# Block-sparse attention and mixture of experts: two loads and stores issued from another queue, and an exponential that permutes while it reads

## The chip, the cores and the metric

The kernel runs on one core of one Trainium2 chip. The metric is the time of one execution on the device in microseconds (us); smaller is better. Every time below comes from runs on the chip or from the trace of one profiled execution.

## The reference

Two computations in a row. First an attention over blocks of 32 positions, with a mask made of a window, the first and last block, and three blocks drawn for each query block; then a layer in which each of the 3072 tokens goes through one of eight experts. All is fp32.

```
B, H, S, D = 4, 8, 768, 64;  block = 32;  n_blocks = 24
mask = |blk_i - blk_j| <= 1, or blk_i or blk_j is the first or the last block
mask[qb*32:(qb+1)*32, kb*32:(kb+1)*32] = True  for the 3 sampled kb of each qb
scores = where(mask, q @ k^T / sqrt(D), -1e9) - max
attn = exp(scores);  attn /= attn.sum + 1e-9;  attn = attn @ v
x = attn as (3072 tokens, 512)
logits = x @ w_gate + modality_bias[modality_id];  e = argmax;  gate_w = softmax(logits)[e]
out = gate_w * (relu(x @ w1[e]) @ w2[e])          # w1 512x1024, w2 1024x512
```

## The kernel before

**Stages.** Up to about 250 us runs the attention, after that the experts, in groups of 256 tokens. The attention has dense rows (first and last query block, lines 360 to 450) and 22 sparse steps: a step g = half*11 + m takes two batches ("half") and the query blocks 2m+1 and 2m+2, and works through items ("s", half, m, n, b), n the query block of the two and b the batch of the two.

**One item** is a chain over four engines. `scores` (L505, TensorE) multiplies 32 queries with eight key blocks: window, first and last, and three drawn ones. `masked` (L513, VectorE) adds the mask and finds the row's minimum, into `y` and `mn`. `exps` (L521, ScalarE) computes exp in two calls of 256 columns, into `a`. `transposed` (L531, TensorE) turns `a` in pieces of 128 columns, and `copied` (L536) brings them out of PSUM. `weigh_shared` (L553) multiplies with the v blocks that both query blocks of the step see, `weigh_own` (L562) with those of one query block alone, the drawn ones among them. `divide` (L435 to L437, VectorE) writes the token rows `xr`; `turned` (L569, L571) and `gate` (L579, L582) make the logits, and `write` (L317, L322) puts `xr` with its gate sum into the DRAM tensor `x_d`, from which the experts gather their tokens later.

**Order of columns.** `y` holds, per half c of 128 columns, the columns in the order (s, f): slot s of four key blocks, position f of 32. v lies on the partitions in the order (f, s), since `vbuf` is viewed as `"(f s) c x -> f s c x"`. Somewhere between, (s, f) has to become (f, s); that happens in `exps`.

**Loads.** Everything from DRAM is fetched ahead by hand. SyncE (SP in the profile) issues `fetch_v` (L479: v of the first and last block, in the first two steps of a half; L480, L481: v of window blocks, 256 KB each), `fetch_own` (L490 reads the drawn block numbers into registers, L493 then issues six loads of 128 KB a step), `dense_q`, `dense_k`, `dense_v` (L146, L153, L159), the experts' weights (L682, L686), `fetch_q` (L141, `q_raw`, one 256 KB load a step, three buffers) and the `x_d` stores of `write` (L322, two of 256.5 KB a step). L322's rows come from `xr` in sparse steps and from `xrd` in dense ones.

**What sets the order.** The order on each engine is the order in which the code is run: a list START for the beginning, then a loop over ticks in which each item's operations come LAG ticks after its start; loads are hooked in at fixed places (`KL`, `QP`, `VL`, `VG`). `write` is a generator that is advanced a little each tick; LATER = 15 idle advances lie between its reciprocal (L317) and its two stores (L322). An engine runs its instructions in order; one that waits holds all behind it.

**Completion semaphores.** A transfer issued by SP or ACT signals its landing on one of eight semaphores, DMAHW0 to DMAHW7, which are given out in turn over both queues. The next transfer on the same semaphore carries a wait for the landing of the one before, whichever queue that was issued from. In the rows of order below, `[waits DMAHW6_49]` is such a wait; PE, DVE and Pool in these brackets stand for results of those engines.

Of the kernel before, what the change touches and what calls it, by code (L numbers as in the profile page):

```python
# [20 lines left out]
P = 128  # L21
# [66 lines left out]
def attention_moe(ctx, tc, kD, qD, qH, v0, v1, blocks, modality, w_gate, bias, w1, w2, out):  # L88
    nc = tc.nc
# [4 lines left out]
    x_d = dram.tile([NTOK, HD + 1], F32, name="x_d")  # L94
# [22 lines left out]
    with ExitStack() as actx:  # L117
# [20 lines left out]

        def fetch_q(half, m):
            q_raw = work.tile([P, 2, HB * NPAIR * 32], F32, name="q_raw", bufs=3)  # L140
            nc.sync.dma_start(q_raw.rearrange("p n f -> p (n f)"), qH[half, m])  # L141
            return q_raw.rearrange("p n (u q) -> p u n q", q=32)

        def dense_q(half):
# [165 lines left out]
        def write(tau, xrs):  # L310
            gs = small.tile([P, 2], F32, name="gs")
            nc.vector.tensor_reduce(gs, exs.pop(tau), axis=AX.X, op=ALU.add)
            yield
            nc.vector.tensor_scalar(gs, gs, 1e-9, None, ALU.add)
            yield
            for n in range(2):
                nc.vector.reciprocal(xrs[n][:, HD:HD + 1], gs[:, n:n + 1])  # L317
            yield
            for _ in range(LATER):
                yield  # L320
            for n in range(2):
                nc.sync.dma_start(x_d[(tau + n) * P:(tau + n + 1) * P, :], xrs[n])  # L322

        def rank(t0_, t1_):
            n = t1_ - t0_
# [192 lines left out]
        def exps(total, y, mn):  # L518
            a = work.tile([P, 768], F32, name="a", bufs=5)[:, 0:512].rearrange("p (u k) -> p u k", u=2)
            for u in range(2):  # L520
                nc.scalar.activation(a[:, u, :].rearrange("p (c f s) -> p c s f", c=2, s=4), y[:, u, :].rearrange("p (c s f) -> p c s f", c=2, s=4),  # L521
                                     AF.Exp, bias=mn[:, u:u + 1], scale=-1.0, accum_out=total[:, u:u + 1])
            return a

# [64 lines left out]
        def routing(tau, lg, pair):  # L589
            yield from route(tau, lg, pair)  # L590
            if tau + 2 < NT:
                yield from write(tau, pair)
                yield from chain(tau + 2)
                return
            both = [chain(tau + 2), write(tau, pair)]
            while both:
                for g in list(both):
                    try:
                        yield next(g)
                    except StopIteration:  # L600
                        both.remove(g)
# [485 lines left out]
        xrs, turns, banks, sums, ats, gated = {}, {}, {}, {}, {}, set()  # L1087
# [19 lines left out]
        for k, it in enumerate(sparse[0] + sparse[1]):  # L1107
            items.append(it)
            if k in DENSE_AFTER:
                c = 2 * DENSE_AFTER.index(k)  # L1110
# [38 lines left out]
        def q_load(m, half):  # L1149
            qraw[m, half] = fetch_q(half, m)  # L1150
# [9 lines left out]
        for g in range(2 * NM):  # L1160
            half, m = divmod(g, NM)
# [19 lines left out]
        def do(op, it):  # L1181
# [29 lines left out]
            else:  # L1211
# [6 lines left out]
                elif op == "M":  # L1218
                    st[it] = masked(m, n, b, st[it])
                elif op == "X":  # L1220
                    if (n, b) == (0, 0):
                        sums[m, half] = small.tile([P, 4, 2], F32, name="sums", bufs=4)
                    st[it] = exps(sums[m, half][:, 2 * b + n, :], *st[it])
                elif op == "T":
                    st[it] = transposed(n, st[it])
                elif op == "A":
                    if n == 0:
                        ats[m, half, b] = work.tile([P, 16, 2, 32], F32, name="at", bufs=NAT)
                    copied(n, b, st.pop(it), ats[m, half, b])
                    if (n, b) == (1, HB - 1):  # L1230
                        sums[m, half] = spread(sums[m, half])
                elif (n, b) == (1, HB - 1):
                    if op == "W":
                        st[it] = bank()
                        weigh_shared(half * NM + m, st[it], [ats[m, half, b_] for b_ in range(HB)])
                    elif op == "V":
                        banks[m, half] = bank()
                        sum_rows(sums.pop((m, half)), banks[m, half])
                        weigh_own(half * NM + m, st[it], [ats[m, half, b_] for b_ in range(HB)])
                    elif op == "O":  # L1240
                        new_tile(m, half)
                        divide(st.pop(it), banks.pop((m, half))[:, 0:H], slice(0, P), H, xrs[m, half][:, 0:HD])
                    elif op == "Y":
                        turns[m, half] = turned(xrs[m, half])
                    elif op == "G":
                        end_tile(m, half)
# [94 lines left out]
```

## Time and profile before

| | |
|---|---|
| median of 3 runs | 559.29 us (558.52 to 562.44) |
| the profiled execution | 560.91 us |
| its span, first to last instruction | 559.2 us |
| mean granted TensorE clock | 0.980 |
| TensorE (PE) busy | 519.0 us, 93% |
| VectorE (DVE) busy | 370.7 us, 66% |
| ScalarE (ACT) busy | 348.2 us, 62% |
| GpSimd (POOL) busy | 182.7 us, 33% |
| DMA traffic | 124.68 MB, 223 GB/s on average |

The span lies inside the execution; 1.7 us are outside it. Times in the profile count from the span's start. SyncE has no row of busy time, as it only issues transfers; its rows are named SPq, and the length of such a row is the time that the queue took to issue the transfer, not the time until the data has landed.

### The profile page before, as it was taken

To read this page: it belongs to the slowest core of one execution; us is meant where nothing else is said; L and a number is where in the kernel's file an instruction comes from. 1 tells how busy PE (TensorE), PEld (TensorE's weight loads), DVE (VectorE), ACT (ScalarE), POOL (GpSimd) and SP (SyncE) were. 2 spreads that over 40 slices of the span, in tenths; PEclk is the share of its full clock that TensorE was granted. 3 is DMA by queue.
4 is the path that set the end of the run, shared out by engine and by line. 5 is a ranking of instruction groups with operands and counts; after the bars stand their busy time and mean duration, and the time that the engine had idled before them with its cause. 6 is when DMAs were issued, how large, how long until landed. Compare 5 with 4: busy or idle time off the path is not lost.

```text
span 559.2 us, 18870 instructions
## 1 busy us (share of the span) xinstructions
PE 519.0 (93%) x7274; PEld 435.4 (78%) x7274; DVE 370.7 (66%) x1151; ACT 348.2 (62%) x746; POOL 182.7 (33%) x413
## 2 busy tenths in 40 slices
PE   6899989999889986889999999999999999999992
PEld 4577767677667664679888898989989899898971
DVE  4796767687678874976986556655566555665560
ACT  3789966987868965862564545545455454554560
POOL 1745526352546542403334330320303203032030
PEclk9999989999999996989999999999999999999997
DMA  8865878777657768857677975767757567575720
GB/s 281 296 197 188 278 227 260 248 248 255 192 163 211 211 193 295 249 169 264 201 239 251 308 250 186 263 193 240 238 190 260 194 228 246 194 259 190 236 105 22
DMA packets 48691, 124.68 MB, mean 223 GB/s; under 512 B 7376, under 2 KB 7504, under 8 KB 48592
## 3 DMA queue, kind: packets, MB, share of 16 engines
q1 hardware_dynamic: 44512, 110.26, 61.4%
q0 software_dynamic: 4080, 13.12, 6.5%
q8 instruction: 59, 0.97, 0.7%
q14 instruction: 40, 0.33, 0.2%
HBM read 110.76 MB, written 12.86 MB: 221 GB/s over the span
## 4 chain that ended last, share of the span: by engine, by line
PE 76%; DVE 7%; DMA 5%; issue 4%; SPq 3%; ACT 2%; POOL 1%; POOLq 0%; DVEq 0%
PE bank L731 8%; PE bank L714 8%; PE bank L730 8%; PE bank L729 8%; PE bank L715 8%; PE bank L716 8%; PE bank L505 7%; PE bank L531 6%; DMA slot<-v 4%; PE bank L553 3%; PE bank L562 3%; PE bank L579 2%; PE bank L703 2%; DVE y L513 1%; PE bank L569 1%
## 5 line engine op out<-in xcount | busy, mean ns | idle before, releaser
L691 DVE TENSOR_TENSOR slot<-slot 128x1024 fp32r<-128x1024 f32 x96 | 120.8, 1264 | 102.8 <-ACT slot L690 98.2
L690 ACT CAST slot<-slot 128x1024 fp32r<-128x1024 f32 x104 | 108.0, 1049 | 109.4 <-PE bank L731 47.1
L521 ACT ACTIVATE a<-y,mn 128x256 f32<-128x256 f32 x176 | 119.5, 779 | 5.2 <-DVE mn L513 5.1
L714 PE MATMUL bank<-slot 128*128 128x256 f32 x384 | 108.4, 282 | 0.0
L716 PE MATMUL bank<-slot 128*128 128x256 f32 x384 | 107.7, 281 | 0.0
L715 PE MATMUL bank<-slot 128*128 128x256 f32 x384 | 107.6, 280 | 0.0
L740 POOL DMA_INDIRECT out<-slot,si x21 | 21.2, 1011 | 182.5 <-ACT slot L736 179.4
L731 PE MATMUL bank<-slot 128*128 128x512 f32 x200 | 79.2, 396 | 1.1 <-DVE slot L722 1.1
L729 PE MATMUL bank<-slot 128*128 128x512 f32 x200 | 80.0, 400 | 0.0
L730 PE MATMUL bank<-slot 128*128 128x512 f32 x200 | 79.1, 395 | 0.0
L469 POOL COPY slot<-slot 128x128 f32 x264 | 64.5, 300 | 26.8 <-issue 26.7
L714 PEld LDWEIGHTS bank<-slot 128*128 128x128 f32 x384 | 72.2, 188 | 0.6
L715 PEld LDWEIGHTS bank<-slot 128*128 128x128 f32 x384 | 72.1, 188 | 0.5
L716 PEld LDWEIGHTS bank<-slot 128*128 128x128 f32 x384 | 72.2, 188 | 0.0
L513 DVE CUSTOM_DVE_ANT_1 y<-bank,smask 128x256 f32<-128x256 f32 x176 | 66.3, 417 | 1.3 <-PE bank L505 0.6
L531 PE MATMUL bank<-ident,a 128*128 128x128 f32 x352 | 54.7, 284 | 6.1 <-DVE mn L513 5.6
L505 PE MATMUL bank<-slot,q_raw 64*32 64x256 f32 x1408 | 51.4, 388 | 3.3 <-DMA q_raw<-qH 2.6
L531 PEld LDWEIGHTS bank<-ident,a 128*128 128x128 f32 x352 | 38.7, 142 | 12.2 <-DVE mn L513 5.0
L731 PEld LDWEIGHTS bank<-slot 128*128 128x128 f32 x200 | 37.6, 188 | 11.0 <-DVE slot L722 2.0
L536 ACT COPY at<-bank 128x512 f32<-128x512 f32 x66 | 38.8, 589 | 9.7 <-PE bank L531 9.6
L730 PEld LDWEIGHTS bank<-slot 128*128 128x128 f32 x200 | 37.6, 188 | 8.1 <-DVE slot L691 0.4
L729 PEld LDWEIGHTS bank<-slot 128*128 128x128 f32 x200 | 37.6, 188 | 7.8 <-ACT slot L889 0.3
(290 smaller groups left out, 817.2 us busy)
## 6 DMA issues: line engine op xcount, KB each, us to landing
slot<-w SPq DMA_DIRECT2D x105, 512.0 KB
slot<-v SPq DMA_DIRECT2D x140, 128.0 KB
slot<-v SPq DMA_DIRECT2D x44, 256.0 KB
slot<-v SPq DMA_DIRECT2D x8, 768.0 KB
x_d<-xr SPq DMA_DIRECT2D x22, 256.5 KB
q_raw<-qH SPq DMA_DIRECT2D x22, 256.0 KB
slot<-kD SPq DMA_DIRECT2D x7, 768.0 KB
x_d<-xrd SPq DMA_DIRECT2D x2, 256.5 KB
```

What stands on the lines that cost most here:

```text
L505: nc.tensor.matmul(sp[u][32 * pr:32 * pr + 32, b * 256:(b + 1) * 256], lhsT=q[r, b * NPAIR + pr, n, :], rhs=kv[r, s0:s0 + 8, b, pr, :], st ...
L513: nc.vector.tensor_tensor_reduce(y[:, u, :].rearrange("p (s f) -> p s f", s=8), sp[u][:, b * 256:(b + 1) * 256].rearrange("p (s f) -> p s ...
L521: nc.scalar.activation(a[:, u, :].rearrange("p (c f s) -> p c s f", c=2, s=4), y[:, u, :].rearrange("p (c s f) -> p c s f", c=2, s=4), AF. ...
L531: nc.tensor.transpose(tp[:, k:k + P], a[:, u, c * P:(c + 1) * P], ident)
L690: nc.scalar.copy(h, staged(n))
L691: (eng or (nc.gpsimd if n in POOL_SPLITS else nc.vector)).tensor_tensor(l, staged(n), h.bitcast(F32), ALU.subtract)
L714: nc.tensor.matmul(o, lhsT=h[:, fs], rhs=xh[g % 2][:, c, :], start=c == 0 and f % 2 == 0, stop=False)
L715: nc.tensor.matmul(o, lhsT=h[:, fs], rhs=xl[g % 2][:, c, :], start=False, stop=False)
L716: nc.tensor.matmul(o, lhsT=l[:, fs], rhs=xh[g % 2][:, c, :], start=False, stop=c == 3 and f % 2 == 1)
L729: nc.tensor.matmul(o, lhsT=hh[0][:, f, ts_], rhs=h[:, fs], start=f == 0, stop=False)
L730: nc.tensor.matmul(o, lhsT=hh[0][:, f, ts_], rhs=l[:, fs], start=False, stop=False)
L731: nc.tensor.matmul(o, lhsT=hl[f // 4][:, f % 4, ts_], rhs=h[:, fs], start=False, stop=f == 7)
```

## The change

Three lines. `fetch_q` issues its 22 loads of `q_raw` from ScalarE's queue (`nc.scalar`) and no longer from SyncE's; `write` does the same with its 24 stores into `x_d`. `exps` makes the order (f, s) on its input: it now reads `y` with a step of 32 elements (every slot's element f, then the next f) and writes `a` in one run, where before it read `y` in one run and wrote `a` with a step of four elements. 176 instructions have this form.

```diff
@@ def fetch_q(half, m):
-            nc.sync.dma_start(q_raw.rearrange("p n f -> p (n f)"), qH[half, m])
+            nc.scalar.dma_start(q_raw.rearrange("p n f -> p (n f)"), qH[half, m])
@@ def write(tau, xrs):
             for n in range(2):
-                nc.sync.dma_start(x_d[(tau + n) * P:(tau + n + 1) * P, :], xrs[n])
+                nc.scalar.dma_start(x_d[(tau + n) * P:(tau + n + 1) * P, :], xrs[n])
@@ def exps(total, y, mn):
-                nc.scalar.activation(a[:, u, :].rearrange("p (c f s) -> p c s f", c=2, s=4), y[:, u, :].rearrange("p (c s f) -> p c s f", c=2, s=4),
+                nc.scalar.activation(a[:, u, :].rearrange("p (c f s) -> p c f s", c=2, s=4), y[:, u, :].rearrange("p (c s f) -> p c f s", c=2, s=4),
                                      AF.Exp, bias=mn[:, u:u + 1], scale=-1.0, accum_out=total[:, u:u + 1])
```

The instructions of TensorE, VectorE and GpSimd keep their order. On SyncE's and ScalarE's queues three places show what moves.

**Place A, near 60 us.** SyncE before, the loads of own v (L493) and window v (L480, L481) around the first two stores:

```order
L493 DMA slot<-v 32x1024 [waits DMAHW0_49]
L493 ISA
L493 DMA slot<-v 32x1024 [waits DMAHW1_49]
L493 ISA
L493 DMA slot<-v 32x1024 [waits DMAHW2_49]
L480 DMA slot<-v 32x2x1024 [waits DMAHW3_49,PE_49]
L481 DMA slot<-v 32x2x1024 [waits DMAHW4_49]
L322 DMA x_d<-xrd 128x513 [waits DMAHW5_49,DVE_49]
L322 DMA x_d<-xr 128x513 [waits DMAHW6_49,DVE_49]
L141 DMA q_raw<-qH 128x512 [waits DMAHW7_49]
```

SyncE after, the same L493 group and the one before it:

```order
L480 DMA slot<-v 32x2x1024 [waits DMAHW4_49,PE_49]
L481 DMA slot<-v 32x2x1024 [waits DMAHW5_49]
L490 TENSOR_LOAD rb_i
L493 ISA
L493 DMA slot<-v 32x1024 [waits DMAHW6_49]
L493 ISA
L493 DMA slot<-v 32x1024 [waits DMAHW7_49]
L493 ISA
L493 DMA slot<-v 32x1024 [waits DMAHW0_49]
L146 DMA qd<-qD 128x512 [waits DMAHW1_49]
L153 DMA slot<-kD 128x1536 [waits DMAHW2_49]
```

ScalarE after, where before the row of L571 was followed by four of L521 with no transfer among them:

```order
L571 COPY xT<-bank 128x512 [waits PE_49]
L521 ACTIVATE a,sums<-y,mn 128x256 [waits DVE_49] x2
L322 DMA x_d<-xrd 128x513 [waits DMAHW6_49,DVE_49]
L322 DMA x_d<-xr 128x513 [waits DMAHW7_49,DVE_49]
L141 DMA q_raw<-qH 128x512 [waits DMAHW1_49]
L521 ACTIVATE a,sums<-y,mn 128x256 [waits DVE_49,Activation_49]
```

The two stores left SyncE and stand on ScalarE between two exponentials. They have places 6 and 7 in the turn of semaphores, and in it they come ahead of SyncE's first two L493 rows of the group on DMAHW6 and DMAHW7, which in the old program were issued ahead of the stores. The query load has DMAHW1 ahead of SyncE's L146.

**Place C, near 138 us.** SyncE after, own v (L493) and v of the first and last block (L479) for the first step of the second half:

```order
L493 DMA slot<-v 32x1024 [waits DMAHW0_49]
L493 ISA
L493 DMA slot<-v 32x1024 [waits DMAHW1_49]
L493 ISA
L493 DMA slot<-v 32x1024 [waits DMAHW2_49]
L479 DMA slot<-v 32x1024 [waits DMAHW3_49,PE_49]
L479 DMA slot<-v 32x1024 [waits DMAHW4_49]
L480 DMA slot<-v 32x2x1024 [waits DMAHW5_49,PE_49]
```

ScalarE after, at the same place:

```order
L413 COPY slot<-bank 128x256 [waits PE_49]
L571 COPY xT<-bank 128x512 [waits PE_49]
L322 DMA x_d<-xr 128x513 [waits DMAHW2_49]
L322 DMA x_d<-xr 128x513 [waits DMAHW4_49]
L396 ACTIVATE a,sm<-bank,nb__3514 128x512 [waits DVE_49,Activation_49]
```

Before, the stores stood on SyncE eight transfers behind these L479 rows (L480, L481, six of L493); now they stand on ScalarE, and the third L493 (DMAHW2) and the second L479 (DMAHW4) follow them in the turn.

**Place E, near 242 us.** SyncE after, the window and own v of the last sparse step:

```order
L493 DMA slot<-v 32x1024 [waits DMAHW5_49]
L480 DMA slot<-v 32x2x1024 [waits DMAHW6_49,PE_49]
L481 DMA slot<-v 32x2x1024 [waits DMAHW7_49]
L490 TENSOR_LOAD rb_i
L493 ISA
L493 DMA slot<-v 32x1024 [waits DMAHW0_49]
```

ScalarE after (L707 rounds an expert's input):

```order
L536 COPY at<-bank 128x16x32 [waits PE_49]
L707 CAST slot<-bank 128x512 [waits PE_49,Pool_49]
L322 DMA x_d<-xr 128x513 [waits DMAHW6_49]
L322 DMA x_d<-xr 128x513 [waits DMAHW7_49]
L707 CAST slot<-bank 128x512 [waits PE_49]
L521 ACTIVATE a,sums<-y,mn 128x256 [waits DVE_49] x2
```

Before, the stores stood on SyncE between the third and the fourth L493 of this step, behind L480 and L481; now L480 and L481 follow them in the turn.

## The prediction

> **What bounds the kernel now.** I read the page first, its busy times and the chain that ended last, and then TensorE's busy time by stretch.
>
> ```profile
> PE 519.0 (93%) x7274; PEld 435.4 (78%) x7274; DVE 370.7 (66%) x1151; ACT 348.2 (62%) x746; POOL 182.7 (33%) x413
> PE 76%; DVE 7%; DMA 5%; issue 4%; SPq 3%; ACT 2%; POOL 1%; POOLq 0%; DVEq 0%
> 30.00:90.00 60.00, 56.24 (x1392) 42.87 (x1392) 43.95 (x214) 53.96 (x159) 30.15 (x105) 0.97 0.72 233
> 90.00:150.00 60.00, 57.11 (x1388) 42.84 (x1386) 44.10 (x201) 50.00 (x146) 23.65 (x81) 1.00 0.74 234
> 150.00:210.00 60.00, 53.40 (x1434) 41.39 (x1430) 45.61 (x239) 48.47 (x142) 31.54 (x109) 1.00 0.68 198
> 210.00:250.00 40.00, 31.68 (x758) 25.27 (x762) 29.06 (x143) 26.41 (x69) 10.62 (x17) 0.83 0.78 245
> 250.00:280.00 30.00, 30.00 (x271) 26.87 (x262) 24.07 (x80) 13.49 (x21) 9.60 (x7) 1.00 0.67 222
> ```
>
> In a stretch's row stand its length and the busy time of PE, PEld, DVE, ACT and POOL, then the granted clock, the DMA share and GB/s. After 250 us TensorE has no gap; the experts' part is untouched by the change. So the change is decided between 30 and 250 us, where TensorE idles 3.8 + 2.9 + 6.6 + 8.3 = 21.6 us: no gain there can be larger, and any lateness beyond the slack of single transfers moves everything behind it. ACT is busy 53.96 + 50.00 + 48.47 = 152.4 of the 180 us from 30 to 210, so it has 27.6 us to spare. What TensorE waited for, and the longest pieces of the chain that are not TensorE's own:
>
> ```profile
> PE bank L562 <- DMA slot<-v: 5.7, 3, 2.9
> PE bank L505 <- DMA q_raw<-qH: 2.6, 1, 2.6
> PE bank L406 <- ACT a L396: 1.6, 3, 1.1
> 65.31 0.51 SPq L322
> 66.35 0.48 SPq L141
> 66.87 2.82 SPq L490
> 79.87 6.16 DMA slot<-v
> 150.47 4.58 DMA q_raw<-qH
> 187.64 3.88 DMA slot<-v
> ```
>
> In the first three rows stand the total, the times and the longest. From 65 us the chain runs down SyncE's queue, issue by issue, into a load of v. So SyncE's queue is nearly the bound, and the kernel lives on v and q that land just in time. The last three rows give what a transfer takes until it has landed: 4.58 us for 256 KB, 3.88 us for 128 KB.
>
> **Part 1, issues leave SyncE.**
>
> ```profile
> L141 SPq DMA_DIRECT2D q_raw<-qH x22: 430/577/1538, 16.6 to 218.6; - x22
> L322 SPq DMA_DIRECT2D x_d<-xr x22: 332/468/1503, 65.9 to 276.8; - x22
> L322 SPq DMA_DIRECT2D x_d<-xrd x2: 528/532/537, 65.3 to 185.1; - x2
> ```
>
> 22 x 0.577 + 22 x 0.468 + 2 x 0.532 = 24.1 us of issue (medians) leave SyncE, about 1.5 us a step. The trace shows no issue by ACT. Nothing leaves ACT by this, so the lower end is 0 (hidden behind a running instruction); as the upper I take SyncE's price, 24.1 us, and of it some 20 up to 210 us. I reckon with the upper end, as SyncE's rows are the nearest: it goes into the 27.6 us to spare, though barely, and costs the end nothing; if that room is used up, see the third rival.
>
> **Part 2, the shared semaphores.** In the order rows, a load on SyncE that follows a moved store in the turn of eight waits until that store has landed, and the store stands at ACT's place. That a load waits for a landing it has no use for stands in the trace of before already:
>
> ```profile
> SPq L479 <- DMA slot<-v: 1.5, 1, 1.5
> ```
>
> No data ties L479 to another load of v; only the turn does. Before, the turn followed SyncE's own order, and the landing waited for was eight transfers old. Now it may be one that ACT has not reached. Place A:
>
> ```profile
> 57.92 1.88 SPq L493 DMA_DIRECT2D slot<-v  x3
> 61.08 2.67 SPq L493 DMA_DIRECT2D slot<-v  x3
> 65.28 0.54 SPq L322 DMA_DIRECT2D x_d<-xrd  x1
> 60.11 0.84 ACT L521 ACTIVATE a<-y,mn 128x256 f32<-128x256 f32 x1
> 60.74 0.80 ACT L521 ACTIVATE a<-y,mn 128x256 f32<-128x256 f32 x1
> 67.19 1.14 PE L562 MATMUL bank<-slot,at 128*32 128x64 f32 x64
> ```
>
> ACT's order puts the stores between two pairs of exponentials here, so they are issued at 60.7 at the earliest (after 59.5 and 60.1's). Landing takes 4.58, as for the load of the same size: 65.3. SyncE's group of three, at 57.92 before, starts there, and the rest of the step's v is issued behind it: the second group ended at 61.08 + 2.67 = 63.75, now 65.3 + (63.75 - 57.92) = 71.1. Its landing took until 67.2 at most (L562 started), 3.4 after; so L562 can start at 74.5 and not at 67.2: **7.3 us late**. Place C:
>
> ```profile
> 132.19 1.86 SPq L493 DMA_DIRECT2D slot<-v  x3
> 138.49 0.60 ACT L571 COPY xT<-bank 128x512 f32<-128x512 f32 x1
> 138.96 0.71 ACT L396 ACTIVATE a<-bank,nb__3514 128x512 f32<-128x512 f32 x1
> 140.25 1.08 PE L562 MATMUL bank<-slot,at 128*32 128x64 f32 x64
> ```
>
> The stores stand between these two ACT rows: issued at 139.0, landed at 143.5; the third L493 behind it is issued by 144.0 and lands 3.88 later at 147.9, where L562 used it at 140.25: **7.6 us late**. Place E:
>
> ```profile
> 241.58 1.05 ACT L707 CAST slot<-bank 128x512 fp32r<-128x512 f32 x2
> 237.02 1.32 SPq L480 DMA_DIRECT2D slot<-v  x1
> 238.40 0.64 SPq L481 DMA_DIRECT2D slot<-v  x1
> 240.56 1.89 SPq L493 DMA_DIRECT2D slot<-v  x3
> 243.88 2.81 SPq L493 DMA_DIRECT2D slot<-v  x3
> 249.41 1.21 PE L562 MATMUL bank<-slot,at 128*32 128x64 f32 x64
> 250.55 0.39 PE L714 MATMUL bank<-slot 128*128 128x256 f32 x1
> ```
>
> The stores stand between the two L707: issued at 242.1 and 242.6 (0.47 apart), landed at 246.7 and 247.2. L480 goes out 246.7 and not 237.02, 9.7 late; L481 at 248.0, and the six L493 behind it need, as before, from 240.56 to 246.69 with the stores' own 0.94 in it, 5.2. With the 1.5 us for L490 (from 238.40 + 0.64 to 240.56) they end at 248.6 + 1.5 + 5.2 = 255.3, and land 249.41 - 246.69 = 2.7 later at 258.0: **8.6 us late**, of which I take 7.6, as ACT's exponentials may give a little.
>
> Each is lateness of its own: a hold is counted from ACT's place, and ACT is moved along by the lateness of the place before. The three give 22.5. Seven more pairs of stores stand in the attention, and 22 query loads hold likewise (L146 in place A). I count the queries' holds with the stores'. For each pair the ends are 0 (its v isn't needed so soon) and place A's 7.3; I take 1.5, nearer to 0, because SyncE gains 1.5 us a step by part 1 and gets ahead that far: 7 x 1.5 = 10.5. The query's own wait of 2.6 goes, as loads of q leave at ACT's place, and what is late next is v, counted already. Sum: 22.5 + 10.5 = **33 us**. With 0 and with half of 7.3 for the seven, 22 and 48.
>
> **Part 3, the exponential.**
>
> ```profile
> L521 ACT ACTIVATE a<-y,mn 128x256 f32<-128x256 f32 x176 | 119.5, 779 | 5.2 <-DVE mn L513 5.1
> 139.64 0.49 ACT L397 ACTIVATE a<-bank,nb__3514 128x256 f32<-128x256 f32 x1
> 140.09 0.61 ACT L536 COPY at<-bank 128x512 f32<-128x512 f32 x1
> ```
>
> Two exponentials of 256 start 60.74 - 60.11 = 0.63 apart with the stepped write; L397, 256 columns written in one run, lets the next start after 140.09 - 139.64 = 0.45. The step thus costs up to 0.18. A stepped read is nowhere in the trace; the ends are 0.45 (free) and 0.81 (twice the surcharge), and I take 0.63, the nearest row of the same line. At 0.45 ACT gains 176 x 0.18 = 32 us, off the bound: TensorE waited for ACT in small pieces only (1.6 us in the largest row), and with the holds ACT has more time yet.
>
> The Trainium skill, page "SBUF — State Buffer", "Door 1: The DMA port swizzle", note on cachelines, has lines of 16 bytes, and each access that crosses to a new line pays. By it the old write (16 bytes on) and the new read (128 bytes on) cross at each element alike and the price stays, so the sum stays 33. The 779 ns of the page's row against L397's 490 ns agree for the write; no run here shows the read.
>
> **The rivals.**
>
> *SyncE is relieved and the holds cost nothing.* ACT would have to reach each store long before SyncE's load comes up. For it: the chain of 65 to 80 us on SyncE's queue, and the 5.7 + 2.6 us of waits above. Then up to 8.3 us go: 553. Against it: the places above, where SyncE's load stood ahead of ACT's place by 2.8 us (A), 5.6 (C) and 5.1 (E).
> The Trainium skill, page "DMA: Bandwidth & Descriptors", "Issuing engines are not separate DMA queues", speaks for this rival no further than that: transfers from several engines share the same 16 engines, and only the issue time is saved. The issue rows of 577 and 468 ns agree; no run here shows ACT's.
>
> *The holds are paid, but once.* If what SyncE loses at A is still slack at C and E (v is fetched up to a step ahead), only the dearest place counts: about 8 us, less 1 to 8 gained: 561 to 569.
>
> *The new read is dear.* At 0.81, ACT has 32 us more from 30 to 250, some 27 of it before 210, and the issues of part 1: 152.4 + 27 + 20 = 199 in 180 us. ACT becomes the bound and adds up to 19 us beside the holds: 594 + 19 = 613. It decides from 0.05 us an exponential on: 27.6 to spare less 20 of issues, over some 152 exponentials up to 210.
>
> **How the numbers follow.** The forecast is 560.9 + 33 = 594 in the profiled execution's terms, 1.6 us over the median of the runs shown, which is less than the bounds here. Chances: holds paid at most places 0.70 (570 to 610), paid once 0.13 (of it 0.05 within 1%), relieved 0.07 (0.06 faster, 0.01 within 1%), dear read 0.10 (600 to 625). A difference under 1%, 5.6 us, can't be told from none here. Faster 0.06, same 0.06, slower 0.88. The range goes from 567, inside "paid once", to 614, inside the dear read; outside lie the relieved case, half of the once-paid one and the top of the dear one, together below 0.2.
>
> **What would show it.** In the changed kernel's trace: SyncE's L493 near 58 us starts after a store of x_d that ACT issued has landed, 7 us later against its own step; TensorE's waits for v grow from 5.7 us to about 30, at L562 and L553 above all; the first L714 after the attention, at 250.55 before, comes near 284; the experts' part stays as long as it was. L521's mean stays near 779. I would be wrong if SyncE's loads don't wait for ACT's stores, if they do but v has more slack than at A, C and E, or if L521's time moves by more than 0.15.

## The result, and the profile after

The changed kernel takes 591.64 us (median of 4 runs, 588.9 to 595.3) against 559.08 (4 runs): a ratio of 1.056, interval 1.050 to 1.061. It is 32.6 us slower; the forecast was 594. The profiled execution took 592.43 us, its span is 590.7. All ratios here and below leave out executions that took over 1.5% more than the fastest of their kernel, and three of the profiles below (both executions with the other turn, before and changed, and both moves to GpSimd) are of such executions, so they are read for who waits for whom and set against each other, not against the rest.

The page of the changed kernel, busy times and chain:

```profile
PE 530.2 (90%) x7274; PEld 444.5 (75%) x7274; DVE 369.8 (63%) x1151; ACT 367.7 (62%) x746; POOL 180.5 (31%) x413
PE 62%; DMA 13%; ACT 8%; DVE 7%; issue 4%; SPq 3%; POOL 0%; ACTq 0%; POOLq 0%; DVEq 0%
```

DMA had 5% of the chain and now has 13%. To see where the time went, the trace is cut at the first L714, the end of the attention: at 250.55 before, 280.93 after. The stretches of before, then of after, with the busy times as in the prediction's table:

```profile
0.00:250.55 250.55, 221.87 (x5324) 169.17 (x5325) 182.90 (x886) 194.29 (x555) 108.26 (x356) 0.97 0.74 232
250.55:559.20 308.65, 297.12 (x1958) 266.23 (x1950) 187.83 (x266) 153.94 (x192) 74.44 (x57) 0.99 0.65 215
```

```profile
0.00:280.93 280.93, 231.52 (x5324) 176.67 (x5325) 185.47 (x891) 215.14 (x556) 109.81 (x357) 0.93 0.66 207
280.93:590.70 309.77, 298.63 (x1953) 267.83 (x1950) 184.30 (x261) 152.56 (x190) 70.67 (x57) 0.98 0.63 215
```

The experts' part grew by 1.1 us, the attention by 30.4. Of these, TensorE's idle time makes 49.4 - 28.7 = 20.7, and 9.7 are TensorE itself, busy longer with the same 5324 matmuls at a granted clock of 0.93 and not 0.97. What TensorE and SyncE waited for in the changed kernel, in total, times and the longest:

```profile
PE bank L562 <- DMA slot<-v: 19.5, 9, 4.8
PE bank L553 <- DMA slot<-v: 2.5, 1, 2.5
SPq L493 <- DMA q_raw<-qH: 25.7, 8, 5.2
SPq L493 <- DMA x_d<-xr: 17.3, 6, 9.7
SPq L480 <- DMA x_d<-xr: 7.0, 2, 6.2
SPq L479 <- DMA q_raw<-qH: 6.3, 2, 5.8
SPq L493 <- DMA x_d<-xrd: 4.9, 1, 4.9
```

L493, L479 and L480 fetch v; none of them uses a query or a stored row. With five smaller rows, SyncE waited 41 us for landings of query loads and 33 us for landings of stores, and none of these rows was there before. Of these 74 us, 21 passed before ScalarE had issued the transfer and 53 between its issue and its landing. TensorE's wait for v at L562 went from 5.7 to 19.5 us; its wait for queries (2.6) is gone.

Place A in the changed kernel, ScalarE's queue, then SyncE's, then TensorE:

```profile
62.55 0.34 ACTq L322 DMA_DIRECT2D x_d<-xrd  x1
63.07 0.66 ACT L571 COPY xT<-bank 128x512 f32<-128x512 f32 x1
60.15 0.64 SPq L481 DMA_DIRECT2D slot<-v  x1
67.22 1.87 SPq L493 DMA_DIRECT2D slot<-v  x3
76.18 1.93 PE L562 MATMUL bank<-slot,at 128*32 128x64 f32 x62 [4.79 <-DMA slot<-v]
```

SyncE was through with L481 at 60.8 and stood until 67.2; ScalarE issued the store at 62.55, and the load goes out 4.7 us later. TensorE then waits 4.79 us for the v of this group.

### The profile page after: what moved, and what is told of

Same layout as the page of the kernel before. It is cut to its first block, busy times and chain, and to the rows that moved or that the text cites. A ratio compares the mean times of both kernels' runs of the same rounds, so it can differ in the third digit from the quotient of the medians.

```text
span 590.7 us, 18874 instructions
## 1 busy us (share of the span) xinstructions
PE 530.2 (90%) x7274; PEld 444.5 (75%) x7274; DVE 369.8 (63%) x1151; ACT 367.7 (62%) x746; POOL 180.5 (31%) x413
## 4 chain that ended last, share of the span: by engine, by line
PE 62%; DMA 13%; ACT 8%; DVE 7%; issue 4%; SPq 3%; POOL 0%; ACTq 0%; POOLq 0%; DVEq 0%
PE bank L714 8%; PE bank L731 8%; PE bank L730 8%; PE bank L715 7%; PE bank L716 7%; PE bank L729 7%; DMA slot<-v 7%; ACT a L521 6%; PE bank L562 3%; DMA x_d<-xr 3%; PE bank L531 3%; DMA q_raw<-qH 2%; PE bank L505 2%; SPq L493 2%; PE bank L703 2%
## 5 line engine op out<-in xcount | busy, mean ns | idle before, releaser
L521 ACT ACTIVATE a<-y,mn 128x256 f32<-128x256 f32 x176 | 132.2, 769 | 0.8 <-DVE mn L513 0.6
L714 PE MATMUL bank<-slot 128*128 128x256 f32 x384 | 109.2, 284 | 0.0
L714 PEld LDWEIGHTS bank<-slot 128*128 128x128 f32 x384 | 73.1, 190 | 0.7 <-issue 0.2
L715 PEld LDWEIGHTS bank<-slot 128*128 128x128 f32 x384 | 73.0, 190 | 0.5
L716 PEld LDWEIGHTS bank<-slot 128*128 128x128 f32 x384 | 73.0, 190 | 0.0
L531 PE MATMUL bank<-ident,a 128*128 128x128 f32 x352 | 56.7, 290 | 6.1 <-DVE mn L513 5.2
L562 PE MATMUL bank<-slot,at 128*32 128x64 f32 x1408 | 31.7, 244 | 23.3 <-DMA slot<-v 19.5
L505 PE MATMUL bank<-slot,q_raw 64*32 64x256 f32 x1408 | 51.0, 388 | 1.0 <-DVE mn L513 1.0
L731 PEld LDWEIGHTS bank<-slot 128*128 128x128 f32 x200 | 37.6, 188 | 11.0 <-DVE slot L722 2.0
L562 PEld LDWEIGHTS bank<-slot,at 128*32 128x32 f32 x1408 | 27.0, 127 | 24.8 <-issue 18.1
```

The costliest lines, as they stand in the source:

```text
L531: nc.tensor.transpose(tp[:, k:k + P], a[:, u, c * P:(c + 1) * P], ident)
L562: nc.tensor.matmul(o[32 * j:32 * j + 32, D * h:D * h + D], lhsT=a[b][:, 8 * u + pr, n], rhs=vg[:, 2 * n, b * HD + D * h:b * HD + D * h + D ...
L714: nc.tensor.matmul(o, lhsT=h[:, fs], rhs=xh[g % 2][:, c, :], start=c == 0 and f % 2 == 0, stop=False)
L715: nc.tensor.matmul(o, lhsT=h[:, fs], rhs=xl[g % 2][:, c, :], start=False, stop=False)
L716: nc.tensor.matmul(o, lhsT=l[:, fs], rhs=xh[g % 2][:, c, :], start=False, stop=c == 3 and f % 2 == 1)
L731: nc.tensor.matmul(o, lhsT=hl[f // 4][:, f % 4, ts_], rhs=h[:, fs], start=False, stop=f == 7)
```

## The experiments

The later runs were made in three groups on three chips, on which the kernel before took some 565 us (its medians there 566.13, 565.23 and 564.92); so each run is compared with the kernel before of its own group, by ratio, and not by its time. The times that the expectations name were set with the 559 us of the first runs in mind. Ratios of different groups differ by the chip too, so a small difference between two of them says less than their intervals do.

| kernel | ratio to before | interval |
|---|---|---|
| the change | 1.056 | 1.050 to 1.061 |
| both moves to ScalarE, exponential as before | 1.052 | 1.041 to 1.062 |
| query loads alone to ScalarE | 1.021 | 1.010 to 1.032 |
| stores alone to ScalarE | 1.043 | 1.035 to 1.051 |
| exponential alone | 1.005 | 0.999 to 1.011 |
| no move, 46 loads of 4 bytes from ScalarE | 1.047 | 1.038 to 1.056 |
| the change, other turn | 1.025 | 1.015 to 1.035 |
| both moves to ScalarE, other turn | 1.023 | 1.015 to 1.032 |
| before, other turn | 1.000 | 0.994 to 1.005 |
| both moves to GpSimd | 0.990 | 0.984 to 0.995 |
| both to GpSimd, and the new exponential | 0.997 | 0.993 to 1.001 |
| stores alone to GpSimd | 0.996 | 0.993 to 1.000 |
| query loads alone to GpSimd | 0.988 | 0.980 to 0.995 |

**The change in two parts.** First the two moves without the exponential:

```diff
-            nc.sync.dma_start(q_raw...)
+            nc.scalar.dma_start(q_raw...)
-                nc.sync.dma_start(x_d[...], xrs[n])
+                nc.scalar.dma_start(x_d[...], xrs[n])
```

> Only the two moves to ScalarE's queue; the exponential as before. Theory A (SyncE's loads are held, through the shared landing semaphores, by transfers that stand at ScalarE's place): nearly the whole loss stays, 583 to 592 us. Theory B (the stepped read makes each exponential some 0.11 us dearer and ScalarE the bound): 557 to 565 us.

And the exponential without the moves:

```diff
-  a[...].rearrange("p (c f s) -> p c s f", ...), y[...].rearrange("p (c s f) -> p c s f", ...)
+  a[...].rearrange("p (c f s) -> p c f s", ...), y[...].rearrange("p (c s f) -> p c f s", ...)
```

> Only the exponential changed; loads and stores on SyncE's queue as before. Theory A: 559 to 564 us, as ScalarE has room between 30 and 250 us for 176 x 0.11 = 19 us more. Theory B: 583 us or more.

1.052 and 1.005: the moves carry the loss, theory A's side in both. (The exponential alone took 568.63 us, above the 559 to 564 of the expectation, but the kernel before took 566.13 on that chip.) The exponential's 0.5% can't be told from nothing by this run alone; see GpSimd below.

**A hold without the transfer.** This is the run that tells a hold from contention. All transfers stay on SyncE, and ScalarE issues beside each a load of four bytes:

```diff
+        tinies = const.tile([1, 46], F32, name="tinies")
+        def tiny():
+            k = left.pop()
+            nc.scalar.dma_start(tinies[:, k:k + 1], kD[0, 0:1, 0, k:k + 1])
         def fetch_q(half, m):
             nc.sync.dma_start(q_raw...)
+            tiny()
 ...
                 nc.sync.dma_start(x_d[...], xrs[n])
+                tiny()
```

> All of SyncE's transfers as before, the exponential too; beside each of the 46 calls ScalarE issues a load of 4 bytes into a scratch row that nothing reads. Theory A (holds through the shared semaphores): SyncE's loads now wait for these loads at ScalarE's place, so the kernel is slower though hardly a byte more is moved: ratio 1.02 to 1.05. Rival C (the loss comes from large transfers in a second queue, their landing or their share of the memory): within 1% of before.

1.047. 46 x 4 bytes cost nearly as much as the two moves with their 12 MB. SyncE's waits, TensorE's largest, and ScalarE's issues (the added lines shift the others: L502 is L493, L148 is the query load L141, L571 is L562), and the two sides of the longest wait:

```profile
SPq L502 <- DMA tinies<-kD: 17.7, 8, 7.1
SPq L148 <- DMA tinies<-kD: 5.4, 1, 5.4
PE bank L571 <- DMA slot<-v: 15.8, 10, 3.1
L144 ACTq DMA_DIRECT2D tinies<-kD x46: 208/209/498, 12.5 to 306.7; - x46
149.43 0.21 ACTq L144 DMA_DIRECT2D tinies<-kD  x1
150.55 1.81 SPq L502 DMA_DIRECT2D slot<-v  x3
```

A v load waits up to 7.1 us for a transfer of four bytes. In this longest wait SyncE stood from 143.4, and ScalarE issued the four bytes at 149.43: 6.0 of the 7.1 us went by until ScalarE came to it, 1.1 on the landing. Rival C (size, landing, memory) is out as a cause by itself: the loss needs no bytes, and from GpSimd's queue the same bytes cost none (below). In the changed kernel the landing is still the larger part of what a hold takes, 53 of the 74 us. That the two ratios come out so close is in part chance: SyncE's waits for the four-byte loads sum to 26 us and not 74, but SyncE keeps its 24.1 us of issues here, and its query loads are held too, so that TensorE waits 11.7 us for queries (2.6 before).

**Another turn.** The framework gives out the semaphores by its own estimate of when each instruction comes up. An option makes it use another estimate:

```diff
-    with tile.TileContext(nc) as tc:
+    with tile.TileContext(nc, schedule_with_timeline_sim=True) as tc:
```

It leaves the attention's order on TensorE and ScalarE as it was (on VectorE and GpSimd a few rows at the very start change places), and in the turn each load of SyncE then stands ahead of the ScalarE transfers that come later in the code. The experts' order changes in part, so there is a yardstick:

> The kernel before, built so that the turn of the eight landing semaphores is given out by another estimate of the order in time (the attention's order on TensorE, VectorE and ScalarE stays, the experts' order changes in part). All transfers are on one queue, so the turn follows that queue as before. Both theories: the attention ends where it did (first L714 at 250 to 252 us); the whole 555 to 566 us, as the experts' order may cost or save a little. It is the yardstick for the next kernel.

> The changed kernel, built with the same other turn: now each load of SyncE stands in the turn ahead of the transfers that ScalarE issues later, so none has to wait for a store or a query load that ScalarE has not reached. Queue, place in ScalarE's order, sizes and the exponential are those of the changed kernel. Theory A: the holds go, the first L714 comes near 250 to 256 us and not near 281, and the time is within 1.5% of the kernel before in the same build. Theory B, or a theory by which transfers from ScalarE's queue are slower or take its time: the loss stays, first L714 at 275 us or later.

The yardstick is at 1.000; its attention ended at 257.15 in the profiled execution, later than the 250 to 252 expected, and its experts' part took 313.5 us where the kernel before takes 308.65. The changed kernel is at 1.025, first L714 at 271.85, 14.7 us behind the yardstick's: about half of the loss goes, and half stays. Theory A's number missed; its reason holds in part. SyncE has no wait for a store or a query load left, and TensorE none for v at L562. But the turn binds both ways; now ScalarE waits, and TensorE for ScalarE:

```profile
ACT slot L413 <- DMA b_raw<-bias: 9.4, 1, 9.4
ACT a L396 <- DMA slot<-v: 4.9, 2, 3.1
ACT a L521 <- DMA qd<-qD: 2.8, 1, 2.8
PE bank L406 <- ACT slot L413: 9.2, 1, 9.2
```

L413 copies a score bank and has nothing to do with the bias; ahead of it in ScalarE's queue stands a query load that waits for the landing of `b_raw`, which is on the same semaphore. Is that the rest of the loss, or the exponential?

> Both moves, the exponential as before, and the other turn of the last kernel. There SyncE was no longer held, but ScalarE waited for landings of SyncE's transfers (9.4 us for b_raw, 4.9 for v, 2.8 for qd), and its exponentials stood in the chain from 201 to 231 us. If the rest of that kernel's loss (ratio 1.025) is these waits of ScalarE alone, 1.02 to 1.03 here too. If the dearer exponential on a ScalarE that now waits is a good part of it, 1.00 to 1.015.

1.023 lies in the range for ScalarE's waits alone, so by this expectation the exponential is not a good part of the rest. In this trace too ScalarE waits at L413 and L396, 8.9 us each:

```profile
ACT a L396 <- DMA slot<-v: 8.9, 3, 4.9
ACT slot L413 <- DMA b_raw<-bias: 8.9, 1, 8.9
```

That these waits make up all of the rest is not shown: the experts' part takes 311.0 and 313.0 us in these two traces, 2 to 4 us more than the 308.65 of before, so a part of both ratios may come from the experts' changed order.

**Queries or stores.** Each move alone (one of the two lines of the first diff):

> Only the 22 query loads move to ScalarE; the stores and the exponential as before. The prediction's sum laid the loss on the stores and counted the queries with them. If that holds: 1.005 to 1.02. By SyncE's waits in the trace of the changed kernel, 41 us of them are for query loads and 33 for stores: then the queries alone make 1.025 to 1.045.

> Only the 24 stores move to ScalarE; query loads and exponential as before. The query loads alone gave a ratio of 1.021 and both moves 1.052. If the holds of stores and of queries add up, the stores alone give 1.02 to 1.035; if a step's lateness is paid once, whichever transfer holds it, 1.035 to 1.05. If the stores cost nothing and the two only hurt together, below 1.01.

The queries alone 1.021, between the two ranges and not settled by the interval; the stores alone 1.043, in the range for a lateness that is paid once; its interval begins at 1.035, where the other range ends. 0.021 + 0.043 = 0.064 is more than both together, 0.052, but the intervals allow that they simply add. Both hold: with the queries alone, SyncE's largest wait is

```profile
SPq L493 <- DMA q_raw<-qH: 22.9, 11, 4.8
```

**A queue with semaphores of its own.** Transfers issued by GpSimd have their own semaphores (in the trace of this run, none of those on which these loads and stores land is used by SyncE); the same two lines with `nc.gpsimd`:

> Both moves, but to GpSimd's queue, whose transfers have semaphores of their own; the exponential as before. SyncE loses the same 24 us of issue and nothing of it waits for a landing in the other queue. Theory A: 0.985 to 1.005, as the holds are gone and the waits for v of 5.7 us shrink, while GpSimd (33% busy) has room for the issues. Rival C (any second queue with these transfers costs as much): 1.03 or more.

0.990, interval 0.984 to 0.995: about 1% faster than before, a small difference that the interval keeps clear of none. The relief of SyncE that the change might have brought is there once the turn is not shared. Waits of TensorE and SyncE, and the issues of query loads on GpSimd:

```profile
PE bank L562 <- DMA slot<-v: 2.2, 2, 2.0
SPq L480 <- PE bank L531: 41.3, 13, 10.8
L141 POOL DMA_DIRECT2D q_raw<-qH x22: 541/586/721, 10.5 to 209.5; - x22
```

SyncE now waits 41.3 us at L480 for a buffer to come free (13.5 before): it is ahead of its work. Which move brings it, and what the exponential costs where nothing is held:

> Only the stores move, to GpSimd's queue. Both moves there gave 0.99. If the gain is SyncE's relief from issues (24.1 us, of it 11.4 for the stores), about half of it stays: 0.99 to 1.00. If it is the stores alone that stood in the way (65 us, chain on SyncE's queue): 0.985 to 0.99.

> Only the query loads move, to GpSimd's queue. By SyncE's relief (12.7 us of issue), 0.99 to 1.00, much as for the stores alone. If the order in which the queries now start (GpSimd's place, ahead of the v loads of the step) delays v: 1.00 to 1.01.

> Both moves to GpSimd's queue and the exponential that reads with a step. No holds, so this shows what the exponential costs by itself: its starts follow 0.74 us apart in the trace of the changed kernel and 0.62 before. ScalarE has some 220 - 179 = 41 us to spare from 30 to 250 in the last kernel, and 152 x 0.12 = 18 us are added: 0 to 6 us over both moves on GpSimd (0.99 to 1.00 of before). If ScalarE is already the bound in places: 1.005 to 1.025.

The stores alone give 0.996, the queries alone 0.988. By their intervals the queries alone are as good as both. The query loads alone lie just below the 0.99 to 1.00 that the issue time gave them, and their interval reaches into that range; whether they gain more than the stores is not settled, and the reason was not tried further. The exponential on top of both moves goes from 0.990 to 0.997, some 4 us, inside the expected 0 to 6; but the two ratios come from different chips, and their intervals touch.

The lowest ratio of these, query loads from GpSimd and the rest as before, is about 1% faster than the kernel before; it can't be told from that of both moves to GpSimd.

## Why the prediction was right, and where its terms were not

*The mechanism.* SyncE's loads wait for ScalarE's transfers through the shared semaphores, v comes late, TensorE waits at L562 and L553: seen in the trace, and shown by the four-byte loads, by the other turn (the wait goes from SyncE to ScalarE) and by GpSimd's queue (it goes). The attention ends 30.4 us later, forecast 33. That the sum came out so near is in part luck: the forecast was lateness from waits alone, and TensorE's idle time grew by 20.7 us only; the other 9.7 come from a term that the sum didn't have. TensorE's waits for v, forecast to reach about 30, reached 24.5 (19.5 at L562, 2.5 at L553 and 2.5 at L428).

*Places A, C, E.* The stores of C and E, SyncE's loads behind them and TensorE's waits:

```profile
159.32 0.33 ACTq L322 DMA_DIRECT2D x_d<-xr  x1
159.68 0.45 ACTq L322 DMA_DIRECT2D x_d<-xr  x1
151.28 11.53 SPq L493 DMA_DIRECT2D slot<-v  x3
162.91 1.34 SPq L479 DMA_DIRECT2D slot<-v  x2
165.21 1.08 PE L562 MATMUL bank<-slot,at 128*32 128x64 f32 x32 [3.75 <-DMA slot<-v]
266.82 0.81 ACTq L322 DMA_DIRECT2D x_d<-xr  x2
269.39 0.65 SPq L480 DMA_DIRECT2D slot<-v  x1
274.02 1.64 PE L553 MATMUL bank<-slot,at 128*64 128x64 f32 x32 [2.46 <-DMA slot<-v]
279.07 1.93 PE L562 MATMUL bank<-slot,at 128*32 128x64 f32 x62 [1.49 <-DMA slot<-v]
```

The sum's terms were lateness, so they are measured by lateness. TensorE runs the same instructions in the same order in both kernels, and the start of one in the new trace less its start in the old one is how late it is. Around place A, before and then after:

```profile
67.11 0.25 PE L546 MATMUL bank<-rexp,fold 128*32 128x8 f32 x8
70.88 0.64 PE L579 MATMUL bank<-wg_raw,xT 128*64 128x8 f32 x16
70.82 0.25 PE L546 MATMUL bank<-rexp,fold 128*32 128x8 f32 x8
81.50 0.64 PE L579 MATMUL bank<-wg_raw,xT 128*64 128x8 f32 x16
```

| TensorE's row | starts before | starts after | late by |
|---|---|---|---|
| L546, ahead of A | 67.11 | 70.82 | 3.7 |
| L579, behind A | 70.88 | 81.50 | 10.6 |
| L569, ahead of a query's hold | 115.06 | 129.62 | 14.6 |
| L579, behind it | 121.80 | 142.47 | 20.7 |
| L546, ahead of C | 140.16 | 161.08 | 20.9 |
| L505, behind C | 145.12 | 171.09 | 26.0 |
| L579, ahead of E | 245.59 | 270.92 | 25.3 |
| first L714, behind E | 250.55 | 280.93 | 30.4 |

A added 6.9 us (7.3 in the sum), C 5.05 (7.6) and E 5.05 (7.6): 17.0 measured and 22.5 forecast. The waits themselves are shorter than that (4.79 at A, 3.75 at C, 2.46 + 1.49 at E); TensorE also runs slower behind them (last section). Two readings were too dear. The landing was taken as 4.58 us each time, the time of a query load in a chain; at A the load that waits goes out 4.7 us after the store, but at C the third L493 goes out 3.0 us after the first store (159.32), and at E L480 2.6 us after. And the stores were put behind the instructions that stand ahead of them on ScalarE, but its queue issues ahead of the engine's work: at A the store goes out at 62.55, 0.5 us before L571 starts (63.07), and L571 and two exponentials stand ahead of it in the order. By the old trace, where this L571 starts at 59.03, that is 58.5 and not 60.7.

*The other stores and the queries.* 10.5 us for both was too little: 13.4 of the 30.4 us came outside the three places. TensorE was 3.7 us late before ScalarE had issued any store. The largest single piece, 6.1 us near 130, starts with a query's hold:

```profile
128.40 0.34 ACTq L141 DMA_DIRECT2D q_raw<-qH  x1
127.92 5.38 SPq L493 DMA_DIRECT2D slot<-v  x3
136.43 1.93 PE L562 MATMUL bank<-slot,at 128*32 128x64 f32 x62 [4.00 <-DMA slot<-v]
```

Between two of these three v loads SyncE stood 3.6 us, until the query load had landed. Query loads alone cost 1.021, some 12 us; I saw that they hold (L146 in place A) and did not price them apart. The 1.5 us for each of the seven pairs leaned on SyncE gaining 1.5 us a step, and that was misread too: there are 24 stores in 22 steps, about one a step and not two, so 24.1 us of issue are 1.1 a step.

*A term that was missing.* No part of the sum let TensorE itself become slower; it is 9.7 of the 30.4 us (last section). The lateness of the places above has a part of it inside. (That TensorE has no gap after 250 us was read from a row that ends at 280; over the whole experts' part it idles 11.5 us before and 11.1 us after, so nothing hangs on it.)

*Issues on ScalarE.* Taken at SyncE's price and as no cost to the end. They take less, and they go out while ScalarE computes (62.55 above lies inside an exponential):

```profile
L141 ACTq DMA_DIRECT2D q_raw<-qH x22: 334/340/475, 12.5 to 238.9; - x22
L322 ACTq DMA_DIRECT2D x_d<-xr x22: 326/361/1336, 63.0 to 309.4; - x22
```

*The exponential.* Taken at 0.63 us from start to start, bounded by 0.45 and 0.81. Two in a row, and the page's row, in the changed kernel:

```profile
56.39 0.81 ACT L521 ACTIVATE a<-y,mn 128x256 f32<-128x256 f32 x1
57.13 0.81 ACT L521 ACTIVATE a<-y,mn 128x256 f32<-128x256 f32 x1
L521 ACT ACTIVATE a<-y,mn 128x256 f32<-128x256 f32 x176 | 132.2, 769 | 0.8 <-DVE mn L513 0.6
```

0.74 from start to start; the mean of one fell from 779 to 769 ns while the busy time rose from 119.5 to 132.2. I had named the mean staying near 779 as the sign of an unchanged price, and that was the wrong number to look at: instructions overlap, and the pitch or the group's busy time shows what one costs its engine. The rival of the dear read was right about the direction, and too high in price: 0.2% to 0.8% of the time by the four pairs of kernels above, which all point the same way, though none is clear of the noise alone. By its own rule the read should have cost more from 0.05 us an exponential on, and it rose by 0.12; but that rule counted the issues as ScalarE's time.

*The rivals.* SyncE's relief is real, but it shows only where no turn is shared (0.990). "Paid once" fell for the change as a whole: A, C and E each made TensorE later.

## What to carry to other kernels

Moving transfers to another queue is not free of the first queue: where both draw their completion semaphores from one turn, each can be held by the other, and a transfer of four bytes is enough. Look at the waits of the built program, not at the diff, and look at the trace for a load that waits for a landing of data it doesn't use. If a queue has to be relieved, a queue with semaphores of its own did it here, for about 1%.

## What the runs showed of the hardware

*A wait costs more than its length.* The stretch after TensorE's wait at place A, in the changed kernel:

```profile
66.00:72.00 6.00, 5.36 (x134) 3.87 (x118) 4.06 (x21) 6.00 (x15) 3.78 (x14) 1.00 0.52 153
72.00:78.00 6.00, 1.82 (x62) 1.71 (x62) 0.00 (x0) 2.53 (x8) 3.40 (x14) 0.59 0.83 293
```

The granted clock falls from 1.00 to 0.59, and 62 matmuls of L562 take 1.93 us where 64 took 1.14 before. In the attention the granted clock is at half in three stretches before and in seven after. Their length and TensorE's busy time in them, summed, before and then after:

```profile
sum 17.06, PE 12.44; mean PE 4.15
sum 37.19, PE 28.91; mean PE 4.13
```

TensorE worked 16.5 us more at half clock; if all of it took twice as long there, that is 8.2 of the 9.7 us, an estimate from above, as the 62 matmuls took less than twice their time. Each of the seven stretches follows a wait of TensorE of 2.2 to 5.2 us that began 1.7 to 4.2 us earlier; five of the seven waits are at L562 and L553, two are for VectorE. That the waits cause the half clock is argued from this order, not tried, and two waits, of 2.2 and 2.5 us, have no such stretch behind them. The Trainium skill, page "TensorE: Matmul & The Clock Gate", "HAM oscillation — how this bites in real kernels", says that an idle gap of over some 3.4 us brings the clock to half. The wait of 4.79 us and the 0.59 behind it agree in direction; but the half clock began 1.7 us into that wait, and before the change a stretch of half clock follows a wait of only 2.13 us (its end at 78.21, the stretch from 79.05). So here shorter waits were followed by half clock too, and the measurement decides.

*A stepped read is dearer than a stepped write on ScalarE.* 0.74 us from start to start for 256 elements read 128 bytes apart, 0.62 written 16 bytes apart, as medians, and alike in the traces of other runs (0.74 in four with the stepped read, 0.61 to 0.62 in five with the stepped write). The rule on cachelines that the prediction cites from the Trainium skill's page "SBUF — State Buffer", by which both cross a line at each element and the price stays, doesn't give this difference; the measurement decides.
